# Dealing the blocks of K, V, dK and dV to partitions as 16 x 8, with stores per head

## The chip, the cores and the metric

One core of a Trainium2 chip runs the whole program. The metric is the device time of one execution in microseconds (us); medians of several executions are given.

## The reference, cut to what matters

Attention with grouped heads, forward and backward. For each of 32 batches there are 32 query heads of 4 rows (128 query rows in all) and 4 key heads of 2048 rows, all 128 wide, in bf16.

```
B, Hq, Hkv, Sq, Sk, D = 32, 32, 4, 4, 2048, 128
scores = einsum("bhqd,bhkd->bhqk", q, repeat(k)) * D ** -0.5
out = einsum("bhqk,bhkd->bhqd", softmax(scores), repeat(v))
# returned: out, dq, dk, dv for a given grad_out
```

Nearly all of the 136 MB read are K and V (134 MB, read once), and nearly all of the 136 MB written are dK and dV (134 MB). The sum over keys does not care in which order keys stand, so a kernel may put any key row on any partition, as long as K, V, dK and dV agree.

## The kernel before

Each head of K or V (512 KB) is one load into a tile of 128 partitions by 16 rows: partition p holds rows 16p to 16p+15, one piece of 4 KB that is contiguous in memory. Such a piece is called a block here; a head has 128 of them. dK and dV leave in 1 MB stores of two heads each. Loads are issued by SyncE, stores by GpSimd.

```python
    keys = lambda t: t.rearrange("b h (p c) d -> b h p (c d)", c=C)                 # C = 16
    pairs = lambda t: t.rearrange("b (g h) (p c) d -> b g p h (c d)", c=C, h=2)
    k_r, v_r, dk_r, dv_r = keys(k), keys(v), pairs(out_2), pairs(out_3)
    ...
            x = p_.tile([P, C, D], BF16, name="k_sb" if name == "LK" else "v_sb")
            nc.sync.dma_start(out=flat(x), in_=src[b, h])
    ...
        elif name in ("DVs", "DKs"):
            g, = arg
            nc.gpsimd.dma_start(out=(dv_r if name == "DVs" else dk_r)[b, g],
                                in_=t[name[:2], "out", g][:].rearrange("p h c d -> p h (c d)"))
```

The order of all instructions on every engine is fixed at build time by a planner (cut here) that models the engines and the DMA. It spreads a batch over about three periods, so that K and V tiles are loaded well before TensorE transposes them.

## Time and profile before

| | before |
|---|---|
| time, median of 2 | 739.41 us |
| one batch, mean distance of the softmax reciprocals | 22.23 us |
| TensorE busy / idle in "issue" / idle for a DMA | 609.7 / 65.7 / 6.8 us |
| DMA rate over the span | 371 GB/s |
| 4 KB packets: mean of loads, of stores | 165.0 ns, 173.1 ns |
| sum of all 4 KB packets, divided by 16 engines | 692.6 us |

"Issue" is time in which an engine stood idle and waited for nothing that the profile shows. The softmax reciprocal is computed once per batch, so its distance is the period of a batch. A packet is one piece of a DMA, here a block of 4 KB. The last two rows are worked out from the packet records in the trace. The median packet takes 159 ns (the shortest 156), which is 16 x 4096 B / 159 ns = 412 GB/s when all 16 DMA engines work.

The first fence has lines of the page: the busy share of the DMA engines in 40 slices of the span, in tenths; the GB/s of the same slices; and the shares of the engines in the chain of work that ended last.

```profile
DMA  8899999999999999999999999999999999999965
GB/s 304 307 400 378 386 352 394 397 396 381 341 402 403 387 399 399 390 371 407 363 406 391 392 351 377 396 398 382 345 360 353 396 398 345 358 387 409 385 245 219
PE 57%; ACT 22%; issue 13%; DVE 3%; DMA 2%; SPq 1%; POOL 0%; POOLq 0%; DVEq 0%; ACTq 0%
```

The DMA engines are busy nearly all the time, and yet only 2% of the chain is DMA.

The second fence is the list of TensorE's waits: who waited for whom, us in total, times, the longest. L464 transposes K and V, L563 makes the products for dV and dK, L526 those for the output and dQ, and L453 transposes q; in the changed kernel these line numbers are one lower.

```profile
PE psum L563 <- issue: 22.8, 18, 2.4
PE psum L464 <- issue: 20.9, 20, 1.9
PE psum L526 <- issue: 20.6, 20, 2.0
...
PE psum L464 <- DMA k_sb<-in_k_dram: 3.5, 1, 3.5
...
PE psum L453 <- DMA q_sb<-in_q_dram: 2.6, 2, 2.4
```

TensorE hardly ever waits for a load. "Issue" stalls are alike on three lines that read quite different things, which suggests that they are not waits for data.

The third fence shows two stretches in which hardly anything but loads moves: the start, and one in the middle (503 packets of loads, 4 of stores). Columns: stretch, its length, busy us of the engines with instruction counts, granted TensorE clock, DMA share, GB/s.

```profile
5.00:22.00 17.00, 12.52 (x161) 11.31 (x161) 6.07 (x11) 8.93 (x17) 0.00 (x0) 1.00 1.01 400
328.00:333.00 5.00, 4.71 (x140) 3.63 (x140) 4.81 (x7) 4.83 (x9) 3.22 (x6) 1.00 1.03 418
```

Loads alone run at 400 to 418 GB/s.

### The profile page before, as it was taken

To read this page: it belongs to the slowest core of one execution; us is meant where nothing else is said; L and a number is where in the kernel's file an instruction comes from. 1 tells how busy PE (TensorE), PEld (TensorE's weight loads), DVE (VectorE), ACT (ScalarE), POOL (GpSimd) and SP (SyncE) were. 2 spreads that over 40 slices of the span, in tenths; PEclk is the share of its full clock that TensorE was granted. 3 is DMA by queue.
4 is the path that set the end of the run, shared out by engine and by line. 5 is a ranking of instruction groups with operands and counts; after the bars stand their busy time and mean duration, and the time that the engine had idled before them with its cause. 6 is when DMAs were issued, how large, how long until landed. Compare 5 with 4: busy or idle time off the path is not lost.

```text
span 739.9 us, 32391 instructions
## 1 busy us (share of the span) xinstructions
PE 609.7 (82%) x14400; PEld 452.3 (61%) x14400; DVE 578.8 (78%) x753; ACT 589.0 (80%) x944; POOL 169.7 (23%) x294
## 2 busy tenths in 40 slices
PE   6888798878888888887989879888888888888883
PEld 5566575656666666665666566566666656666662
DVE  1878787777887789787888787777778888787892
ACT  3888798887888898887888788787778878787882
POOL 0122221221221222221222221221112222122221
PEclk9999999999999999999999999999999999999996
DMA  8899999999999999999999999999999999999965
GB/s 304 307 400 378 386 352 394 397 396 381 341 402 403 387 399 399 390 371 407 363 406 391 392 351 377 396 398 382 345 360 353 396 398 345 358 387 409 385 245 219
DMA packets 83083, 274.72 MB, mean 371 GB/s; under 512 B 16384, under 2 KB 16384, under 8 KB 82944
## 3 DMA queue, kind: packets, MB, share of 16 engines
q0 software_dynamic: 36864, 136.33, 48.9%
q1 hardware_dynamic: 46080, 136.34, 47.3%
q8 instruction: 112, 1.84, 0.9%
q14 instruction: 27, 0.22, 0.1%
HBM read 136.31 MB, written 136.31 MB: 368 GB/s over the span
## 4 chain that ended last, share of the span: by engine, by line
PE 57%; ACT 22%; issue 13%; DVE 3%; DMA 2%; SPq 1%; POOL 0%; POOLq 0%; DVEq 0%; ACTq 0%
PE psum L464 30%; PE psum L475 9%; PE psum L563 9%; PE psum L526 7%; ACT dk_sb L568 6%; ACT e_sb L491 6%; ACT dv_sb L568 3%; ACT vt_sb L432 2%; PE psum L515 2%; ACT dt_sb L432 1%; DMA k_sb<-in_k_dram 1%; DMA v_sb<-in_v_dram 1%; ACT qdt_sb L432 1%; ACT kt_sb L432 1%; ACT et_sb L432 1%
## 5 line engine op out<-in xcount | busy, mean ns | idle before, releaser
L568 DVE CAST dk_sb<-psum 128x1024 bf16<-128x1024 f32 x128 | 153.6, 1221 | 48.0 <-PE psum L563 45.6
L568 DVE CAST dv_sb<-psum 128x1024 bf16<-128x1024 f32 x128 | 155.8, 1219 | 29.6 <-PE psum L563 22.9
L464 PE MATMUL psum<-ident,k_sb 128*128 128x128 bf16 x2048 | 155.4, 225 | 16.9 <-issue 11.5
L432 ACT COPY kt_sb<-psum 128x512 f32<-128x512 f32 x229 | 131.2, 600 | 38.1 <-PE psum L464 35.4
L464 PEld LDWEIGHTS <-k_sb 128*128 128x128 bf16 x2048 | 122.0, 100 | 55.2 <-issue 38.5
L464 PE MATMUL psum<-ident,v_sb 128*128 128x128 bf16 x2048 | 146.5, 223 | 9.4 <-issue 9.4
L568 ACT CAST dk_sb<-psum 128x1024 bf16<-128x1024 f32 x128 | 127.0, 1024 | 30.5 <-PE psum L563 30.2
L464 PEld LDWEIGHTS <-v_sb 128*128 128x128 bf16 x2048 | 122.5, 100 | 37.4 <-issue 33.2
L568 ACT CAST dv_sb<-psum 128x1024 bf16<-128x1024 f32 x128 | 132.4, 1035 | 13.2 <-PE psum L563 12.8
L432 ACT COPY vt_sb<-psum 128x512 f32<-128x512 f32 x196 | 109.6, 589 | 36.2 <-PE psum L464 35.9
L548 DVE SCALAR_TENSOR_TENSOR ds_sb<-psum,delta,e_sb 128x1024 bf16<-128x1024 f32 x64 | 82.0, 1281 | 17.2 <-PE psum L475 15.3
L572 POOL DMA_DIRECT2D out_dram<-dv_sb x64 | 45.3, 710 | 206.0 <-DVE dv_sb L568 168.8
L563 PE MATMUL psum<-qp_sb,ds_sb 32*128 32x128 bf16 x2048 | 61.2, 217 | 26.7 <-issue 10.5
L563 PE MATMUL psum<-dop_sb,e_sb 32*128 32x128 bf16 x2048 | 61.3, 218 | 18.8 <-issue 12.3
L491 ACT ACTIVATE e_sb<-psum,m 128x1024 bf16<-128x1024 f32 x64 | 72.2, 1129 | 0.6 <-DVE mjunk L482 0.6
L503 POOL TENSOR_SCALAR qp_sb<-q_sb,rinv 128x128 bf16<-128x128 bf16 x32 | 11.7, 366 | 249.1 <-PE psum L563 199.8
L563 PEld LDWEIGHTS <-ds_sb 32*128 32x128 bf16 x2048 | 36.3, 92 | 44.8 <-issue 31.2
L526 PE MATMUL psum<-k_sb,dt_sb 128*32 128x128 bf16 x2048 | 48.3, 224 | 15.3 <-issue 14.7
L563 PEld LDWEIGHTS <-e_sb 32*128 32x128 bf16 x2048 | 34.3, 93 | 36.3 <-issue 20.5
L572 POOL DMA_DIRECT2D out_dram<-dk_sb x64 | 48.2, 753 | 22.6 <-ACT et_sb L432 9.8
L482 DVE TENSOR_SCALAR_CACHE_REDUCE mjunk<-psum,m 128x1024 bf16<-128x1024 f32 x32 | 41.1, 1283 | 11.3 <-PE psum L475 10.1
L515 PE MATMUL psum<-ident,ds_sb 128*128 128x128 bf16 x512 | 39.5, 220 | 10.7 <-DVE ds_sb L548 10.2
(74 smaller groups left out, 643.5 us busy)
## 6 DMA issues: line engine op xcount, KB each, us to landing
k_sb<-in_k_dram SPq DMA_DIRECT2D x128, 512.0 KB, 8.6
v_sb<-in_v_dram SPq DMA_DIRECT2D x128, 512.0 KB, 9.8
out_dram<-dv_sb POOLq DMA_DIRECT2D x64, 1024.0 KB, 8.1
out_dram<-dk_sb POOLq DMA_DIRECT2D x64, 1024.0 KB, 9.5
q_sb<-in_q_dram SPq DMA_DIRECT2D x32, 32.0 KB, 9.5
go_sb<-in_grad_out_dram SPq DMA_DIRECT2D x32, 32.0 KB, 7.0
out_dram<-o_sb POOLq DMA_DIRECT2D x32, 32.0 KB, 10.3
out_dram<-dq_sb POOLq DMA_DIRECT2D x32, 32.0 KB, 7.6
```

The costliest lines, as they stand in the source:

```text
L432: nc.scalar.copy(out=out.rearrange("p c d -> p (c d)").bitcast(FP32), in_=in_.rearrange("p c d -> p (c d)").bitcast(FP32))
L464: nc.tensor.transpose(out=ps[:, j, :], in_=t[x, h][:, 8 * i + j, :], identity=ident[:])
L475: nc.tensor.matmul(t[name, i][r, QW * w:QW * w + QW], lhsT=t["qdt"][:, side, r], rhs=t[x, h, i][:, CPQ * w:CPQ * w + CPQ, :], start=True, ...
L482: nc.vector.tensor_scalar(out=junk[:], in0=t["S", i][:], scalar1=-scale, scalar2=t["m"][:] if i else None, op0=ALU.mult, op1=ALU.min, accu ...
L491: nc.scalar.activation(out=t["e"][:, 2 * QW * i:2 * QW * i + 2 * QW], in_=t["S", i][:], func=ACT.Exp, bias=t["m"][:], scale=scale, accum_o ...
L503: nc.gpsimd.tensor_scalar(out=t["qp"][:], in0=t["q"][:], scalar1=t["rinv"][:], scalar2=scale, op0=ALU.mult, op1=ALU.mult)
L515: nc.tensor.transpose(out=ps[:, j, :], in_=src[:, P * c:P * c + P], identity=ident[:])
L526: nc.tensor.matmul(t[name][r, 0:D], lhsT=t[xt, c // 8][:, c % 8, r], rhs=t[x, h][:, c, :], start=(c == 0), stop=(c == C - 1), tile_positio ...
L548: nc.vector.scalar_tensor_tensor(out=t["ds"][:, w], in0=t["DP", i][:], scalar=t["dl"][:], in1=t["e"][:, w], op0=ALU.subtract, op1=ALU.mult)
L563: nc.tensor.matmul(accs[h // 2][:, w:w + P], lhsT=t[lhs][r, P * c:P * c + P], rhs=t[rhs][r, :], start=True, stop=True, tile_position=(32 * ...
L568: copy(out=t[name[:2], "out", g][:, :, CPQ * i:CPQ * i + CPQ, :].rearrange("p h c d -> p h (c d)"), in_=t[name[:2], i][g][:].rearrange("p ...
L572: nc.gpsimd.dma_start(out=(dv_r if name == "DVs" else dk_r)[b, g], in_=t[name[:2], "out", g][:].rearrange("p h c d -> p h (c d)"))
```

## The change

The intent: at any moment the 16 DMA engines should work on neighbouring 4 KB blocks of memory. Block number 16j + e goes to partition 8e + j, so the memory side of a DMA becomes 16 (step one block) x 8 (step 16 blocks). The stores are cut per head; for two heads the pattern would need one dimension more.

```diff
-    keys = lambda t: t.rearrange("b h (p c) d -> b h p (c d)", c=C)
-    pairs = lambda t: t.rearrange("b (g h) (p c) d -> b g p h (c d)", c=C, h=2)
+    keys = lambda t: t.rearrange("b h (j e c) d -> b h e j (c d)", c=C, e=16)
-    k_r, v_r, dk_r, dv_r = keys(k), keys(v), pairs(out_2), pairs(out_3)
+    k_r, v_r, dk_r, dv_r = keys(k), keys(v), keys(out_2), keys(out_3)
...
-            nc.gpsimd.dma_start(out=(dv_r if name == "DVs" else dk_r)[b, g],
-                                in_=t[name[:2], "out", g][:].rearrange("p h c d -> p h (c d)"))
+            for h in range(2):
+                nc.gpsimd.dma_start(out=(dv_r if name == "DVs" else dk_r)[b, 2 * g + h],
+                                    in_=t[name[:2], "out", g][:, h, :, :].rearrange("p c d -> p (c d)"))
```

## The prediction

> **What bounds the kernel now.** The page shows the 16 DMA engines in tenth 9 of nearly every slice (371 GB/s), so it looks DMA-bound. I think it is not. In the list of waits of TensorE, loads appear only at the start (k_sb 3.5 us once, q_sb 2.6 us, go_sb 0.7 us); VectorE and ScalarE never wait for a store to free an output buffer. The chain of work that ended last is PE 57%, ACT 22%, issue 13%, DVE 3%, DMA 2%, and its only large DMA pieces are v_sb 6.97 us and k_sb 9.23 us before 21.7 us. Putting each load's landing beside the first transpose that reads it (batches 4 to 29), k tiles land 3.0 us or more before their use (median 5.6), v tiles 1.9 us or more (median 9.2). So the steady state (about 22 us a batch, 32 batches) is paced by TensorE's fixed instruction order, its hand-offs with ScalarE and VectorE, and by "issue" stalls in the middle of groups (66 us of TensorE idle time, about 60 stalls of up to 2.4 us), which I take for instruction fetch: 112 packets of 16 KB, mean 0.96 us each. DMA just keeps up, with small slack.
>
> **What the change does.** TensorE, VectorE and ScalarE keep their instructions and order; bytes and 4 KB packets are the same.
> - Placement: [...] Packets have a floor of 159 ns; stores average 173 ns, loads 165 ns: 29 + 12 us of 16-engine time above the floor. Much of it sits in store-only bursts of 4 to 5 us, with packets near 300 ns. [...]I expect loads unchanged and perhaps half of the store excess gone: some 15 us of DMA time.
> - Stores per head: 256 issues instead of 128 on GpSimd. A 1 MB issue took 0.71 to 0.75 us, a 32 KB one 0.58 us, so I estimate 0.6 to 0.7 us for a 512 KB one: 65 to 85 us more GpSimd busy (170 to about 245 us), in stretches where GpSimd idles 5 to 7 us.
>
> **On the critical path.** Saved DMA time only lengthens slack. I count 0 to 5 us from shorter fetch stalls and tail, 0 to 1 us of loss from the later last issue.
>
> **Prediction.** 737 us, 8 in 10 between 727 and 748. Faster by over 2%: 0.09; within 2%: 0.82; slower by over 2%: 0.09.
>
> **What would show each step.** Right: TensorE's waits hold almost no DMA; batch period 22 us; "issue" near 13% of the chain; store packets nearer 159 ns, landing times shorter, time unmoved; GpSimd busy near 245 us with nobody waiting for it. Wrong: PE waiting for k_sb or v_sb, or a period that follows the DMA.
>
> **What would make it wrong.** Slower: if the new pairing of partitions with engines makes engines collide (on HBM or on the SBUF side), packets above about 175 ns would eat the 2 to 5 us of slack and the DMA would become the bound: room is about 6%. Faster: if fetch stalls are mostly queueing behind slow store packets, up to 15 us would come back; or if some waits called "issue" are hidden waits for DMA.

"Loads unchanged" and "half of the store excess gone: some 15 us of DMA time" stand as the author's estimate. 739.4 us of before, less 0 to 5 us and plus 0 to 1 us, was put at 737 us; the 15 us of DMA time were not in it, as they were taken to lengthen slack only.

## The result, and the profile after

The changed kernel is correct and takes 823.77 us (median of 2, 822.79 to 824.75) against 739.41 us. The ratio is 1.114, 95% interval 1.107 to 1.122. Ratios here are the mean time of one kernel's fast runs over that of the other's fast runs of the same rounds, so they are not quite the ratio of the medians quoted.

The same lines of the page after:

```profile
DMA  8999999999999999999999999999999999999874
GB/s 193 229 352 346 354 357 326 359 383 316 376 334 348 348 336 372 345 388 338 361 353 318 378 327 372 316 340 372 305 389 367 360 348 324 334 390 349 284 242 161
PE 49%; DMA 16%; issue 14%; ACT 13%; DVE 5%; POOL 1%; SPq 1%; POOLq 0%; DVEq 0%; ACTq 0%
```

The DMA row is as full as before, but it moves less per slice (193 instead of 304 GB/s in the first), and DMA has entered the chain with 16%. A busy row does not tell how fast the engines are; the GB/s row below it does.

TensorE's waits after:

```profile
PE psum L463 <- issue: 37.2, 18, 4.3
PE psum L562 <- issue: 35.5, 17, 4.7
PE psum L525 <- issue: 17.4, 16, 2.7
PE psum L463 <- DMA k_sb<-in_k_dram: 16.4, 11, 5.5
...
PE psum L463 <- DMA v_sb<-in_v_dram: 3.6, 4, 1.3
```

Load-only stretches after, columns as before:

```profile
5.00:30.00 25.00, 11.95 (x132) 9.86 (x131) 4.71 (x8) 8.72 (x16) 0.00 (x0) 1.00 1.03 240
321.00:325.00 4.00, 3.37 (x89) 2.27 (x78) 3.81 (x6) 3.68 (x6) 2.38 (x5) 1.00 1.03 282
345.00:349.00 4.00, 3.77 (x92) 2.82 (x92) 3.67 (x6) 3.48 (x7) 1.86 (x4) 1.00 1.01 267
```

This is the symptom: where loads run alone, in the stretches shown, they run at 240 to 282 GB/s instead of 400 to 418. Their packets take 238 to 278 ns on average in these stretches, against 160 to 163 ns in the stretches shown of before. Where loads and stores run together, the median packet stays at 159 ns (loads 170 and 163 ns on average at 316 to 320 and 340 to 344 us).

Where the 81 us between the two profiled spans (739.9 and 821.0 us) went, from the softmax reciprocals (one per batch) in the two traces:

```
                            before    after    difference
start to first reciprocal    22.0      32.7      +10.7
31 batch periods            22.23     24.33      +65.1  (31 x 2.10)
last reciprocal to the end   28.8      33.9       +5.1
```

And as TensorE saw it: 34.0 us more busy (609.7 to 643.7), 28.4 us more idle in "issue" (65.7 to 94.1), 16.8 us more idle for DMAs (6.8 to 23.6).

More busy with the same instructions goes with a slower clock here: the granted clock (the share of TensorE's full clock that it was given) fell from 0.976 to 0.926. How one long stall costs time twice is seen in the chain of work after, in order of time (start, length, what), and in the two stretches around it:

```profile
128.01 0.16 PE psum L463
128.17 4.34 issue
132.51 3.40 PE psum L463 x31
```

```profile
128.00:132.50 4.50, 0.17 (x4) 0.05 (x2) 1.54 (x2) 1.16 (x2) 0.00 (x0) 0.98 1.01 331
132.50:136.00 3.50, 3.49 (x43) 3.36 (x46) 0.69 (x1) 1.23 (x3) 0.00 (x0) 0.54 1.03 412
```

TensorE stands still for 4.34 us, its clock is granted at 0.54 afterwards, and 31 transposes take 3.40 us; undisturbed groups of 32 on the same line take 1.89 us elsewhere in the chain. The clock records show 27 stretches at half clock in the changed kernel and 8 in the kernel before. Of the 27, three come with pauses of TensorE of 4.21, 4.34 and 4.73 us and one with the end of its work; the other 23, and all 8 of before, follow pauses of 1.3 to 3.3 us (before, for example, 1.88 us at 86.85 us). How long a pause has to be for the clock to fall was not tested.

### The profile page after: what moved, and what is told of

The parts are those of the page before. It is cut to its first block, busy times and chain, and to the rows that moved or that the text cites. A ratio compares the mean times of both kernels' runs of the same rounds, so it can differ in the third digit from the quotient of the medians.

```text
span 821.0 us, 32675 instructions
## 1 busy us (share of the span) xinstructions
PE 643.7 (78%) x14400; PEld 480.0 (58%) x14400; DVE 580.8 (71%) x753; ACT 594.3 (72%) x944; POOL 212.4 (26%) x422
## 4 chain that ended last, share of the span: by engine, by line
PE 49%; DMA 16%; issue 14%; ACT 13%; DVE 5%; POOL 1%; SPq 1%; POOLq 0%; DVEq 0%; ACTq 0%
PE psum L463 26%; DMA k_sb<-in_k_dram 9%; PE psum L562 8%; PE psum L474 7%; PE psum L525 6%; DMA out_dram<-dq_sb 5%; ACT dk_sb L567 4%; ACT e_sb L490 4%; DMA out_dram<-dv_sb 3%; ACT dv_sb L567 2%; PE psum L514 2%; ACT vt_sb L431 1%; DVE dk_sb L567 1%; DVE ds_sb L547 1%; ACT dt_sb L431 1%
## 5 line engine op out<-in xcount | busy, mean ns | idle before, releaser
L463 PE MATMUL psum<-ident,k_sb 128*128 128x128 bf16 x2048 | 176.2, 243 | 41.1 <-issue 23.4
L463 PEld LDWEIGHTS <-k_sb 128*128 128x128 bf16 x2048 | 139.6, 110 | 84.8 <-issue 55.5
L463 PE MATMUL psum<-ident,v_sb 128*128 128x128 bf16 x2048 | 151.2, 226 | 17.5 <-issue 13.8
L463 PEld LDWEIGHTS <-v_sb 128*128 128x128 bf16 x2048 | 126.0, 101 | 49.8 <-issue 40.8
L567 ACT CAST dv_sb<-psum 128x1024 bf16<-128x1024 f32 x128 | 131.9, 1032 | 21.5 <-PE psum L562 20.9
L572 POOL DMA_DIRECT2D out_dram<-dv_sb x128 | 67.0, 530 | 261.6 <-DVE dv_sb L567 213.6
L562 PE MATMUL psum<-dop_sb,e_sb 32*128 32x128 bf16 x2048 | 63.0, 227 | 32.1 <-issue 26.7
L562 PE MATMUL psum<-qp_sb,ds_sb 32*128 32x128 bf16 x2048 | 63.1, 222 | 26.5 <-issue 8.8
L572 POOL DMA_DIRECT2D out_dram<-dk_sb x128 | 68.3, 539 | 22.7 <-ACT et_sb L431 11.7
L434 DVE COPY vt_sb<-psum 128x1024 bf16<-128x1024 bf16 x60 | 41.1, 684 | 20.8 <-PE psum L463 20.4
```

The lines of the kernel that those rows point to most:

```text
L434: nc.vector.tensor_copy(out=out, in_=in_)
L463: nc.tensor.transpose(out=ps[:, j, :], in_=t[x, h][:, 8 * i + j, :], identity=ident[:])
L562: nc.tensor.matmul(accs[h // 2][:, w:w + P], lhsT=t[lhs][r, P * c:P * c + P], rhs=t[rhs][r, :], start=True, stop=True, tile_position=(32 * ...
L567: copy(out=t[name[:2], "out", g][:, :, CPQ * i:CPQ * i + CPQ, :].rearrange("p h c d -> p h (c d)"), in_=t[name[:2], i][g][:].rearrange("p ...
```

## The experiments

Theories at the start. **Stores**: the 128 extra stores cost the time. **Address**: the 16 engines collide in memory when they read neighbouring blocks. **Form**: the addresses do not matter; the outer count of 16 on the memory side changes which partitions each DMA engine fills, or how the descriptors of a DMA are made.

### Which part of the change: k1_heads, k2_loads, k3_stores

k1_heads cuts the stores per head and keeps the layout of before:

```diff
-    k_r, v_r, dk_r, dv_r = keys(k), keys(v), pairs(out_2), pairs(out_3)
+    k_r, v_r, dk_r, dv_r = keys(k), keys(v), keys(out_2), keys(out_3)      # keys of before; stores per head
```

> The layout of before on both sides; only the 1 MB stores of two heads are cut into two stores of 512 KB (128 more issues on GpSimd). If the stores per head cost the time (GpSimd busy 212 us instead of 170 us, later stores), this comes out near 820 us. If the placement of the loads costs it, this stays within 1% of before, 735 to 745 us, with GpSimd busy near 212 us.

k2_loads deals only the loads; k3_stores deals only the stores. Their dK and dV rows are permuted, and those runs fail the comparison for that reason (dK by a relative error of 1.4; dV shows it little, with 0.0068 against 0.0051 in k6_quarter, whose dV rows stand in order).

```diff
+    dealt = lambda t: t.rearrange("b h (j e c) d -> b h e j (c d)", c=C, e=16)
+    k_r, v_r, dk_r, dv_r = dealt(k), dealt(v), pairs(out_2), pairs(out_3)  # k2_loads
+    k_r, v_r, dk_r, dv_r = keys(k), keys(v), dealt(out_2), dealt(out_3)    # k3_stores, per head
```

> Only the loads are dealt; stores as before, in pairs and in natural order (the rows of dK and dV are permuted on purpose, so the check of the result fails for them). If the dealt loads are the cause, this is near the changed kernel, 805 to 830 us, and load packets in load-only stretches take about 245 ns. If the stores are the cause, it stays near 740 us.

> Only the stores are dealt and per head; loads as before (rows of dK and dV permuted on purpose). If the dealt loads are the cause, 735 to 750 us: the stores of the changed kernel have only 13 us more of 16-engine packet time than before, and there is slack for that. If stores are the cause, near 820 us.

| | time, median | ratio to before (95%) | mean packet, loads / stores | packets / 16 | first reciprocal, period |
|---|---|---|---|---|---|
| before | 738.65 us (7 runs) | | 165.0 / 173.1 ns | 692.6 us | 22.0, 22.23 us |
| k1_heads | 741.03 us | 1.005 (0.997 to 1.012) | 167.2 / 170.5 ns | 691.6 us | 21.5, 22.08 us |
| k2_loads | 818.75 us | 1.109 (1.101 to 1.118) | 210.6 / 169.3 ns | 778.0 us | 32.8, 24.27 us |
| k3_stores | 768.27 us | 1.041 (1.033 to 1.049) | 163.3 / 190.1 ns | 723.7 us | 22.6, 22.95 us |
| changed | 823.77 us | 1.114 (1.107 to 1.122) | 201.1 / 179.7 ns | 780.0 us | 32.7, 24.33 us |

(The profile columns of "before" and "changed" are of the first two traces; the time of "before" is that of the rounds of the three experiments. One of its 7 runs, 745.66 us, was slow; the ratios leave it out, and the median of the other six is 738.23 us.)

Cutting the stores costs nothing, although GpSimd was busy for 210.2 us instead of 169.7 us: the store theory is out. Dealt loads alone bring nearly the whole loss. Dealt stores alone bring 4%, which I had expected not to be felt: that expectation failed, and it shows how little slack there was. The two do not add: the time follows the sum of packet times ("packets / 16"), and in the changed kernel that sum is nearly that of k2_loads (780.0 and 778.0 us). Why dealt stores add so little beside dealt loads is not shown.

### Address or form: m1_forms

A kernel without attention runs 28 loads of 512 KB per phase, nothing else in flight, then 28 stores per phase. The memory side is written by hand as (outer count, step, inner count, step), steps in blocks of 4 KB; a phase starts when the one before has landed.

```python
LOADS = dict(a=(128, 1, 1, 0), b=(16, 1, 8, 16), c=(16, 9, 8, 1), d=(16, 1, 8, 17), e=(32, 1, 4, 32), f=(64, 1, 2, 64),
             g=(16, 2, 8, 32), i=(16, 16, 8, 1), j=(16, 129, 8, 16), k=(16, 1, 8, 129))
STORES = dict(s=(128, 1, 1, 0), t=(16, 1, 8, 16), u=(16, 9, 8, 1), w=(16, 129, 8, 16))
```

> No attention, outputs wrong on purpose: ten phases of 28 loads of 512 KB, nothing else in flight, each with another walk through memory, then four phases of 28 stores. Reading mean packet time in each load phase. Form a (128 blocks in order) should be at 159 to 170 ns, form b (the dealt one[...]) near 245 ns. Theory 1, neighbouring addresses collide in HBM: form c (same 16 x 8 shape of the DMA[...]) is fast, near 160 ns, and so are i (64 KB apart) and j (516 KB apart, 64 KB jumps); d and k ([...]jumps of 68 KB and 516 KB) are slow; e and f and g (neighbouring with 8 or 16 KB) lie between. Theory 2, the 16 x 8 shape of the DMA changes which partitions an engine fills or how its descriptors are made: c, d, g, i, j and k are all as slow as b whatever the addresses, about 245 ns. Theory 3, the jump of 64 KB[...]: b, j slow, d and k (68 and 516 KB) fast. Stores: no difference between forms of more than 10% is expected by any.

(Between outer blocks the step in memory is 4 KB in b, d and k and 36 KB in c.)

The stretches inside phases a, b, c, e, f, j and k, in that order (columns: stretch, length, busy VectorE and GpSimd, clock, DMA share, GB/s):

```profile
core 0: us, DVE busy (x) POOL busy (x), PEclk, DMA share, GB/s
3.00:39.00 36.00, 4.38 (x27) 0.00 (x0) 1.00 1.01 402
45.00:100.00 55.00, 4.05 (x25) 0.00 (x0) 1.00 1.03 239
110.00:165.00 55.00, 4.14 (x26) 0.00 (x0) 1.00 1.03 241
...
236.00:272.00 36.00, 4.22 (x26) 0.00 (x0) 1.00 1.02 401
276.00:312.00 36.00, 4.22 (x26) 0.00 (x0) 1.00 1.02 403
...
448.00:502.00 54.00, 4.23 (x26) 0.00 (x0) 1.00 1.03 246
511.00:569.00 58.00, 4.09 (x26) 0.00 (x0) 1.00 1.03 232
```

Every form with an outer count of 16 runs at 232 to 246 GB/s (d, g and i too: 235, 241, 239), whether the outer step is 4 KB (b, d, k), 8 KB (g), 36 KB (c), 64 KB (i) or 516 KB (j), and whatever the inner jump. Packets of form b took 281 ns, somewhat more than the 245 expected. The forms with outer counts 32 and 64 (e, f) run at 401 and 403 GB/s like the plain one, with the same outer step of 4 KB as b. The address theory is out, and with it the theory of the 64 KB jump. It is the outer count of 16.

Of the stores, s ran at 380 GB/s, t at 368 and w at 364, from first packet to last. Form u was spoilt: its stores overlap in memory, and 27 of its 28 stores waited for another store (91.0 us in all), so it says nothing.

### What the outer count changes: m2_parts

m1_forms shows that the outer count of 16 costs the time and leaves open why. The author's guess: it changes which partitions are filled at the same time, and some partitions cannot be filled together at the full rate. If so, sets of partitions must differ in rate even where no DMA has the 16 x 8 form.

The test loads from memory in plain order and changes only the set of partitions filled:

```python
# name: first partition, step, partitions
LOADS = dict(a=(0, 8, 16), b=(0, 1, 16), c=(0, 4, 16), d=(0, 4, 32), e=(0, 1, 32), f=(0, 2, 64), g=(0, 1, 64), h=(0, 1, 128))
```

> Outputs wrong on purpose. Loads of 512 KB from memory in natural order, nothing else in flight; only the set of partitions they fill differs, 28 loads per set. Theory 2a[...]: 16 partitions in a row (form b)[...] the rate is about 105 to 125 GB/s; 16 partitions 8 apart (form a)[...]: 210 to 245 GB/s, as the dealt form; [...]128 (h): 390. [...]Rival 2b, the making of descriptors for a 16 x 8 form is what is slow: a, b, c, d, e, f, g, h all near 390 GB/s, as none has that form. Stores from 128 partitions in forms 128, 16 x 8, 32 x 4, 64 x 2: 16 x 8 a few per cent slower than the other three, which are alike.

The stretches inside phases a to h:

```profile
core 0: us, DVE busy (x) POOL busy (x), PEclk, DMA share, GB/s
5.00:73.00 68.00, 3.96 (x27) 0.00 (x0) 1.00 1.00 202
80.00:210.00 130.00, 4.04 (x27) 0.00 (x0) 1.00 1.01 109
217.00:285.00 68.00, 4.05 (x27) 0.00 (x0) 1.00 0.99 200
291.00:324.00 33.00, 3.75 (x25) 0.00 (x0) 1.00 0.99 407
331.00:398.00 67.00, 4.01 (x27) 0.00 (x0) 1.00 1.02 207
404.00:438.00 34.00, 3.90 (x26) 0.00 (x0) 1.00 0.99 407
444.00:512.00 68.00, 4.00 (x27) 0.00 (x0) 1.00 1.02 206
518.00:551.00 33.00, 3.77 (x26) 0.00 (x0) 1.00 1.02 409
```

The rate goes by which partitions are filled, not by how many: 16 in a row (b) run at 109 GB/s, 16 that are 8 or 4 apart (a, c) at 202 and 200; 32 in a row (e) at 207, 32 that are 4 apart (d) at 407; 64 in a row (g) at 206, 64 that are 2 apart (f) at 407; all 128 (h) at 409. 64 partitions in a row (g) are no faster than 16 partitions eight apart (a). The packets of these sets differ in size (32, 16, 8 and 4 KB for 16, 32, 64 and 128 partitions), but sets of the same size differ in rate too: a 32 KB packet took 4.82 us on average in b and 2.56 to 2.57 us in a and c, a 16 KB one 1.28 us in e and 0.63 us in d. What the partitions of a slow set share is not shown. The rival that puts the cost in making descriptors for a 16 x 8 DMA is not needed here, as none of these loads has that form. The records of m1_forms speak against it too: in form b the engines were busy all the time (DMA share 1.03) with packets of 281 ns, while in two phases of m3_mixed below, in which DMAs are issued too slowly, the share is 0.65 and 0.66 and the median packet takes 159 ns. The dealt form fills all 128 partitions in the course of a DMA, as h does, but runs at 239 GB/s (form b of m1_forms), nearer to the 200 to 207 of a, c, e and g than to the 409 of h. That at any one moment it fills a set that is slow in this way is not shown.

Stores of this kernel: plain 381, 16 x 8 364, 32 x 4 381, 64 x 2 380 GB/s from first packet to last. Again only the outer count of 16 stands out, but by 4% and not by 40%. All loads here are issued by SyncE and all stores by GpSimd, so whether the direction or the issuing engine makes this difference was not tested.

### The same partitions, and loads beside stores: m3_mixed

```python
PHASES = dict(a=((16, 2, 2, 1), 4, None), b=((16, 4, 4, 1), 2, None), c=((16, 5, 4, 1), 2, None), d=((16, 3, 2, 1), 4, None),
              e=(NAT, 1, NAT), f=(DEAL, 1, NAT), g=(NAT, 1, DEAL), h=(DEAL, 1, DEAL))   # loads' form, step of partitions, stores' form
```

In a and b the steps fit together, so the pattern is the same as a plain outer count of 32 and 64; in d and c a gap keeps it at 16.

> Outputs wrong on purpose. a and d: 32 partitions 4 apart, 4 KB each, once with outer count 32 in memory (a) and once as 16 x 2 (d); b and c: 64 partitions 2 apart, outer count 64 (b) and 16 x 4 (c). If an outer count of 16 hands each engine neighbouring partitions[...], d and c are near 205 to 245 GB/s beside a and b at 330 or more (these DMAs are small, so issue may cap them). e to h: 28 loads beside 28 stores, both 512 KB: natural loads and stores (e), dealt loads (f), dealt stores (g), both dealt (h). [...]f within 5% of e, all near 380 to 400 GB/s in total; if dealt DMAs are slow as such, f and h are near 300.

The stretches inside phases b, c, e, f, g and h:

```profile
26.00:45.00 19.00, 3.75 (x25) 0.00 (x0) 1.00 1.00 369
50.00:76.00 26.00, 3.75 (x25) 0.00 (x0) 1.00 1.02 275
103.00:171.00 68.00, 4.05 (x27) 12.66 (x24) 1.00 1.02 417
178.00:247.00 69.00, 4.05 (x27) 12.18 (x23) 1.00 1.03 416
253.00:323.00 70.00, 4.05 (x27) 12.77 (x25) 1.00 1.02 413
329.00:400.00 71.00, 3.90 (x26) 12.09 (x24) 1.00 1.02 408
```

b and c fill the same 64 partitions; the outer count differs (64 and 16), with the gap in memory that keeps it so, and the rate falls from 369 to 275 GB/s. That is less of a fall than expected (205 to 245). It fits that the outer count decides which partitions are filled together. (a and d came out at 203 and 206 GB/s, capped by the issue of such small DMAs: 128 KB every 0.56 us is 233 GB/s. They tell nothing.) Which engine filled which partition is not shown; the packet records do not name the engine.

Beside stores, dealt loads cost next to nothing: 416 against 417 GB/s, and 408 with dealt stores as well (380 to 400 was expected of all four). Loads then move only about half of the bytes, some 205 GB/s, which is below the 239 GB/s that dealt loads reach alone. This is why the changed kernel looks healthy in mixed stretches and loses only where loads run alone, above all in the first 30 us and in the load-only part of each batch.

### One number changed in the kernel: k4_e32, k5_e64

```diff
-    keys = lambda t: t.rearrange("b h (j e c) d -> b h e j (c d)", c=C, e=16)
+    keys = lambda t: t.rearrange("b h (j e c) d -> b h e j (c d)", c=C, e=32)   # k4_e32;  e=64: k5_e64
```

> The changed kernel with one number changed: the 128 blocks of a head are dealt as 32 x 4 instead of 16 x 8, so blocks stay neighbouring[...], stores stay per head, and the result is right. The forms run says a 32 x 4 load runs at 389 GB/s. Theory 2[...]: 732 to 748 us, as before, load packets back to 159 to 170 ns on average. Rival, dealing as such costs: above 790 us.

> The same with 64 x 2[...]. Theory 2: as k4_e32, 732 to 748 us. Rival: between k4_e32 and before, if nearness of addresses matters by degrees.

Both are correct. k4_e32 takes 745.67 us against 742.22 us of before in the same rounds (ratio 1.006, 1.002 to 1.011), k5_e64 744.63 us (1.004, 0.999 to 1.010). Load packets take 166.5 and 168.1 ns on average, store packets 169.9 ns in both, and the period of k4_e32 is 22.00 us. So dealing itself costs about half a per cent (at most 1.1% by the intervals), an outer count of 16 costs 11%, and neighbouring blocks bring no gain: stores of k1_heads, with plain addresses, have 170.5 ns. Two lines of the page of k4_e32, to be read against those of before and after:

```profile
GB/s 288 269 404 381 405 392 380 392 404 387 407 386 375 397 400 394 412 405 380 378 395 408 374 370 339 368 403 409 361 396 364 394 387 379 389 356 393 399 237 132
PE 56%; ACT 17%; issue 11%; DMA 6%; DVE 6%; POOL 1%; SPq 1%; POOLq 0%; ACTq 0%; DVEq 0%
```

### Was there slack in the kernel before: k6_quarter, k7_half

The prediction rested on the DMA not being what paces the kernel. These two leave out stores of before and change nothing else. Their outputs are wrong, which doesn't matter for the times.

```diff
         elif name in ("DVs", "DKs"):
             g, = arg
+            if name == "DVs" or g == 0:     # k6_quarter: three of four stores;  k7_half: if g == 0
-            nc.gpsimd.dma_start(...)
+                nc.gpsimd.dma_start(...)
```

> The kernel before with one of its four 1 MB stores per batch left out (dK of the heads 2 and 3 is never written; wrong on purpose): an eighth of all bytes less, every engine instruction else the same. If the kernel before is paced by its engines and the DMA has slack, as the prediction said, this is 725 to 740 us. If it already ran at the pace of the DMA, so that any added packet time lands in the time, it falls by near an eighth of its 22 us per batch, to 650 to 680 us; between the two, both pace it in turn.

> Two of the four 1 MB stores left out (dV and dK of the heads 2 and 3; wrong on purpose): a quarter of the bytes less. Paced by engines: the same as k6_quarter within 1%, 720 to 740 us. Paced by DMA alone: below 600 us.

| | bytes | time, median | ratio to before (95%) | period | TensorE idle in "issue" | TensorE busy |
|---|---|---|---|---|---|---|
| before | 100% | 738.71 us | | 22.23 us | 65.7 us | 609.7 us |
| k6_quarter | 87.5% | 709.20 us | 0.960 (0.953 to 0.967) | 21.24 us | 43.1 us | 603.1 us |
| k7_half | 75% | 688.65 us | 0.932 (0.927 to 0.937) | 20.55 us | 21.9 us | 598.3 us |

Neither answer of the expectations holds alone, and k7_half is not within 1% of k6_quarter. The time does not fall in proportion to the bytes, so the DMA is not the only pace; but it does fall, so the kernel before already paid for its DMA traffic. Of the 53.5 us between the profiled spans of before (739.9) and k7_half (686.4), 43.8 us are "issue" stalls of TensorE and 11.4 us its busy time. Its list of waits, to be read against that of before:

```profile
PE psum L464 <- issue: 8.9, 10, 1.7
...
PE psum L563 <- issue: 6.5, 11, 1.3
PE psum L526 <- issue: 5.8, 8, 1.7
```

What these stalls are can be read from the packet records. For every "issue" stall of TensorE over 0.3 us, the last instruction packet of 16 KB that had ended before TensorE went on was looked up:

```
            stalls   median stall   from the packet's start to TensorE going on (5% / median / 95%)   packet began after the stall did
before        57       1.15 us       2.23 / 2.39 / 2.54 us                                              0
changed       51       1.66 us       2.31 / 2.54 / 2.78 us                                              16
k6_quarter    45       0.98 us       2.25 / 2.38 / 2.53 us                                              0
k7_half       27       0.72 us       2.23 / 2.41 / 2.53 us                                              0
```

TensorE goes on a nearly constant time after an instruction packet starts, in all kernels. I read the stalls as waits for instructions, whose packets the page counts among those of the 16 DMA engines (before: queue q8, 112 packets, 0.9% of the engines' time); no experiment changed the fetch alone. In the changed kernel a third of these packets begin only after TensorE has run dry. Whether the request itself was late or stood in a queue behind data packets, the records do not tell; that stays open.

### Why dealt stores cost more in the kernel than alone: m4_busy

Alone, dealt stores have packets of 175 ns; in k3_stores 190 ns, with 1% above 665 ns. m4_busy runs plain and dealt stores beside idle engines, then beside ScalarE and VectorE copying, TensorE reading, and all three.

```python
PHASES = [(NAT, ""), (DEAL, ""), (NAT, "AD"), (DEAL, "AD"), (NAT, "P"), (DEAL, "P"), (NAT, "ADP"), (DEAL, "ADP")]
```

> Outputs wrong on purpose. Why dealt stores cost 22 us or more in the kernel (packets 190 ns on average[...]) but only 4% alone (175 ns beside 170 ns). Stores of 512 KB, natural and dealt, with idle engines, with ScalarE and VectorE copying in on-chip memory, with TensorE reading it, and with all three. If the engines' own traffic [...], dealt stores rise from 175 ns to 190 ns or more in the busy phases while natural ones stay within 5 ns of 170. If not, dealt stores stay at 175 ns in all, and the rest of the cost in the kernel stays open.

Mean packets were, plain and dealt: 170 and 175 ns idle, 169 and 175 ns beside copies, 169 and 177 ns beside TensorE, 170 and 175 ns beside all. The engines' own traffic does not explain it, and neither do plain loads beside them (163 ns in phase g of m3_mixed). Why dealt stores reach 190 ns in k3_stores stays open.

## Why the prediction was wrong, point by point

- **"I expect loads unchanged."** This is the step that failed first. The change was costed by memory addresses alone. Load packets went from 165.0 to 201.1 ns on average, and m1_forms shows that addresses have no part in it: outer steps of 36, 64 and 516 KB are as slow as 4 KB. What changed is the outer count of the memory side (k4_e32 and k5_e64 undo the loss with this number alone), and through it perhaps, as m2_parts and m3_mixed suggest, which partitions are filled together. The prediction named a collision "on the SBUF side" as a way to be wrong, but gave it 9% and did not work out from the diff which partitions would be filled together.
- **"Perhaps half of the store excess gone."** Store packets rose to 179.7 ns. With outer counts of 128 and 32, cut per head, stores improve by 3 ns (k1_heads, k4_e32), and nearness has no part in it.
- **"Saved DMA time only lengthens slack" and "room is about 6%".** The landing times were read rightly: 2 to 5 us of slack for the tightest tiles. But slack of a tile is a buffer that is used up once, not a rate. The sum of packets was 692.6 us of a span of 739.9 us; 31 us more of packets (k3_stores) made 30 us more of time (768.27 against 738.65), 87 us more (changed) made 84 us more. In the changed kernel 13 of 128 K tiles and 7 of 128 V tiles land less than 0.2 us before their first use, against 3 and 0 before. And k6_quarter and k7_half show that the DMA was felt even before, mostly through "issue" stalls.
- **"Which I take for instruction fetch"** is borne out by the nearly constant 2.4 us. The conclusion that only 0 to 5 us hang on it was wrong: 44 us of stalls vanish when half of the stores do, and 28 us appear in the changed kernel.
- **GpSimd.** Predicted about 245 us busy, measured 212.4 us, as an issue of 512 KB took 0.53 to 0.54 us and not 0.6 to 0.7 us. That nobody would wait for it was right (k1_heads: ratio 1.005).
- **Not foreseen:** with more and longer stalls TensorE's clock was at half in 27 stretches instead of 8, and the same instructions took 34.0 us longer.

## What to carry to other kernels

When the pattern of a DMA changes, look at two things: the addresses it touches, and the outer count on the memory side; here the first made no difference and an outer count of 16 cost 11%. Keep that count at 32 or more where the tile has 128 partitions (loads with 32, 64 and 128 ran at 401 to 403 GB/s, with 16 at 232 to 246). Where a load fills only some of the partitions, which ones they are matters: 16 in a row ran at 109 GB/s, 16 that are 8 apart at 202. A DMA row that reads 9 everywhere has to be read with the GB/s below it, and slack before one tile's use is no proof that the DMA does not pace the kernel: leave out some stores and see.

No variant beat the kernel before: its plain form already runs at 400 to 418 GB/s when loads run alone, as fast as the fastest sets of m2_parts (407 to 409 GB/s), and dealing with 32 or 64 only matches it.
